# A gated recurrence with routed experts on one core: the first three groups in series, casts in 6 KB runs, the moduli row written transposed

## The chip, the cores and the metric

One core of a Trainium2 chip. The time is device microseconds of one execution of the program; the number given for a kernel is the median of its runs. A profile of one further execution shows which engine worked when.

## What is computed

For each of 4 batches and 8 heads a state of 48 x 48 complex numbers is decayed and turned at each of 768 steps by a gate (a_re, a_im), the outer product of k and v is added, and y is q times the real part. The 32 rows of heads then form x of 3072 tokens by 384, which goes through a top-1 mixture of 8 experts:

```python
mag = np.sqrt(a_re * a_re + a_im * a_im)
scale = np.minimum(mag, 0.999) / (mag + 1e-06)
a_re_n, a_im_n = (a_re * scale, a_im * scale)
for t in range(S):
    new_re = ar * S_re - ai * S_im
    new_im = ar * S_im + ai * S_re
    S_re, S_im = (new_re + k_t outer v_t, new_im)
    y[:, :, t] = q_t @ S_re
...
logits = x @ w_gate + modality_bias[modality_id]
e_idx = np.argmax(logits, axis=1)
out[mask] = gate_w[mask, None] * (np.maximum(x[mask] @ w1[e], 0.0) @ w2[e])
```

## The kernel before

**Units and groups.** The recurrence is cut into 6 chunks of 128 steps. A *unit* is one chunk of one batch with its 8 heads: 24 units, chunk by chunk. Two units make a *group* x (12 of them), and the element-wise work is done per group, on tiles of 128 steps by 768.

**Phases of a group.** `load_a` and `load_qk` (L100, L109) bring the inputs, four DMAs of 192 KB each, rows of 48 floats. `squares` (L116) makes the squared parts, `logs` (L127) their logarithms, `tangents` (L135) the tangent of the gate's angle, `arctans` (L148) the angle. `angles` (L151) sums the angles over the steps by a triangular matmul into PSUM tiles `u`; `fractions` (L171) takes the turns off, after adding the sum of the chunk before (`cb`, brought by `carries`, L162, from a DRAM row `f_scr` which `fractions` writes). `waves` (L193) makes sine and cosine (`cs`). `sums` and `moduli` (L201, L212) do the same with the log moduli and give `pm`. `moduli` also writes the last step's moduli to a DRAM row `m_scr` (L222) and reads it back with head and dimension exchanged, twice, into `mt` (L225), which scales the state.

**Stages of a unit.** `hats` (L232) multiplies q and k by moduli and waves. `turned` (L254) transposes both on TensorE (`tKT`, `tQT`), and ScalarE copies them to SBUF. `inner` (L266) makes the attention matrix (`wp`, then `W` by VectorE). `outer` (L279) makes the state's update (`up`) and the output (`yp`; after the first chunk also from the state, L302). `rows` (L307) transposes the output and computes the gate's logits (`xw`); ScalarE casts it into `xr` (L315), and a DMA writes it to `x_rows`.

**What sets the order.** ScalarE needs one set of function tables for log and exp and another for sine and arctan. `table` loads a set, and `then` chains table loads and activations into one order by hand. The loop over w (L360) interleaves: turn w runs `turned` of unit w + 2, `inner` of w + 1, `outer` of w, `rows` of w - 1, and phases of groups two to six ahead. Even turns use the log set, odd ones the sine set. Before the loop, groups 0 and 1 go through squares, logs and tangents together and then through arctans and angles together; the loop starts at w = -4, so that the first turns only have phases to do. Within this program order the framework's planner places each engine's instructions by when it reckons their inputs to be ready, and puts in the waits. SP issues all plain DMAs in one queue, in order; an instruction that waits holds those behind it.

**Casts.** `cast_weights` (L416) turns each expert's weights to bf16 in DRAM, 16 DMAs issued by GpSimd. `w1b` holds row k*128 + p of w1 in partition p, slot k; `w2b` row c*128 + p of w2. A cast is issued in two of three turns, and waits for a mark two turns back (L400 to L403).

**Experts.** After the router, 19 tiles (12 of 256 tokens, 7 of 128) run in `expert_layers` (L649): weights by DMA, tokens by gather, a transpose, `up` (L693: for each 128 hidden columns three matmuls with weights from `w1t`, into `h_ps`), `down` (L713, `y_ps`), and a scatter.

Of the kernel before, what the change touches and what calls it, by code (L numbers as in the profile page):

```python
# [11 lines left out]
F32 = mybir.dt.float32  # L12
BF16 = mybir.dt.bfloat16
# [6 lines left out]
U32 = mybir.dt.uint32  # L20
# [3 lines left out]
def gate_loop(nc, ctx, tc, cpool, ident, q, k, v, a_re, a_im, sel, lg, x_rows, casts, make_router):  # L24
# [4 lines left out]
    B, H, S, D = q.shape  # L29
    L = 128  # L30
    G = S // L
    J = H // 2
    C = 2 * D
    NG = 2
# [4 lines left out]
    un = ctx.enter_context(tc.tile_pool(name="un", bufs=2))  # L39
# [1 line left out]


    f_scr = nc.dram_tensor("f_scr", (G * B, H * D), F32, kind="Internal").ap()
    m_scr = nc.dram_tensor("m_scr", (G * B, H, D), F32, kind="Internal").ap()

    mask = cpool.tile([L, L], F32, name="mask")
    nc.gpsimd.memset(mask[:], 1.0)
# [14 lines left out]
    def bank(shape, name):  # L62

        full = ps.tile([128, 512], F32, name=name, tag="bank", bufs=7)
        n = 1
        for s in shape[1:]:
            n *= s
        flat = full[0:shape[0], 0:n]
        if len(shape) == 2:
            return flat  # L70
        names = " ".join(f"x{i}" for i in range(len(shape) - 1))
        return flat.rearrange(f"p ({names}) -> p {names}", **{f"x{i}": s for i, s in enumerate(shape[1:])})
# [7 lines left out]
    chain = []  # L80

    def then(ins):
        if chain:
            tc.add_manual_dep(ins.ins, chain[-1].ins.name, mybir.DependencyInfo(mybir.DependencyClass.NoSync, mybir.DependencyReason.DATA), reason="order of the table sets")
        chain.append(ins)

    def table(name):
        then(nc.scalar.preload_act_table_set(name))  # L88

    def act(*args, **kw):  # L90
        then(nc.scalar.activation(*args, **kw))  # L91
# [120 lines left out]
    def moduli(x):  # L212
        ls = box.pop(("sums", x))
        pm = el.tile([L, 2, NG, H, D], F32, name="pm")
        for i in range(NG):
            act(pm[:, 0, i], ls[i], Act.Exp)
            act(pm[:, 1, i], ls[i], Act.Exp, scale=-1.0)
        g, b = groups[x][0]
        if g < G - 1:

            n0 = g * B + b
            nc.sync.dma_start(out=m_scr[n0:n0 + NG].rearrange("i h d -> (i h d)")[None], in_=pm[L - 1:L, 0].rearrange("o i h d -> o (i h d)"))  # L222
            mt = un.tile([C, NG, H], F32, name="mt", bufs=4)
            for c in range(2):
                nc.sync.dma_start(out=mt[c * D:(c + 1) * D], in_=m_scr[n0:n0 + NG].rearrange("i h d -> d i h"))  # L225
            box["mt", x] = mt
        box["pm", x] = pm

    def both(x):
        return x[:, :, None, :].broadcast_to([L, H, 2, D])  # L230

    def hats(w):  # L232

        if not 0 <= w < NU:
            return
        x, i = w // NG, w % NG
        cs = box["cs", x]
        pm = box["pm", x]
        qk = box["qk", x]
        qp = un.tile([L, H, D], F32, name="qp")  # L240
        nc.vector.tensor_tensor(qp[:], qk[:, 0, i], pm[:, 0, i], Alu.mult)
        kp = un.tile([L, H, D], F32, name="kp")
        nc.vector.tensor_tensor(kp[:], qk[:, 1, i], pm[:, 1, i], Alu.mult)
        Kh = un.tile([L, H, 2, D], F32, name="Kh", bufs=5)
        nc.vector.tensor_tensor(Kh[:], cs[:, i], both(kp[:]), Alu.mult)
        Qh = un.tile([L, H, 2, D], F32, name="Qh", bufs=3)
        nc.vector.tensor_tensor(Qh[:], cs[:, i], both(qp[:]), Alu.mult)
        box["hats", order[w]] = Qh, Kh
# [58 lines left out]
    def rows(g, b):  # L307

        yT = box.pop(("outer", g, b))
        xw = bank([L, J, sel.shape[2]], "xw")  # L310
        for j in range(J):
            nc.tensor.matmul(xw[:, j, :], yT[:, j, :], sel[:, j, :], start=True, stop=True)  # L312
        nc.vector.tensor_reduce(lg[:, g * B + b, :], xw[:, :, C:].rearrange("t j e -> t e j"), axis=AX.X, op=Alu.add)
        xr = un.tile([L, J, C], BF16, name="xr")
        nc.scalar.copy(xr[:], xw[:, :, 0:C])  # L315
        n0 = 1 + (b * G + g) * L
        nc.sync.dma_start(out=x_rows[n0:n0 + L, 0:H * D // 2], in_=xr.rearrange("t j c -> t (j c)").bitcast(U32))

    NX = len(groups)
    NU = len(order)  # L320
    EXP, TRIG = "natural_log_exp_and_others", "trig_and_small"
    late = []
    takes = {7: 0, 15: 8, 19: 16, 23: 20}
    done = set()

    def phase(f, x):

        if 0 <= x < NX and (f, x) not in done:
            done.add((f, x))
            f(x)  # L330

    def unit(stage, w):
        if 0 <= w < NU:
            stage(*order[w])


    for x in range(2):
        phase(load_a, x)
    phase(load_qk, 0)
    phase(load_a, 2)  # L340
    table(EXP)
    for x in range(2):
        phase(squares, x)
        phase(logs, x)
        phase(tangents, x)
    table(TRIG)
    for x in range(2):
        phase(arctans, x)
        phase(angles, x)
    phase(fractions, 0)  # L350
    phase(squares, 2)
    phase(load_a, 3)
    phase(waves, 0)
    phase(load_qk, 1)
    phase(fractions, 1)

    rt = None
    open_ = []
    marks = []
    for w in range(-4, NU + 1):  # L360


        even = w % 2 == 0
        x = w // 2
        unit(values, w + 2)
        if even:
            phase(load_a, x + 6)
            phase(carries, x + 4)
            phase(fractions, x + 3)
        else:  # L370
            phase(load_qk, x + 3)
            hats(w + 3)
        unit(turned, w + 2)
        if even:
            if x + 2 < NX:
                table(EXP)
            phase(logs, x + 4)
        elif x + 3 < NX:
            table(TRIG)
            phase(arctans, x + 4)  # L380
        unit(inner, w + 1)
        if even:
            phase(sums, x + 2)
            phase(moduli, x + 2)
            for f in late:
                f(act)
            late.clear()
        unit(outer, w)
        if even:
            hats(w + 3)  # L390
            phase(tangents, x + 4)
        else:
            phase(waves, x + 3)
            phase(squares, x + 5)
        unit(rows, w - 1)
        if not even:
            phase(angles, x + 4)
        if w == 0:
            rt = make_router(ctx, ps, bank)
        marks.append(chain[-1])  # L400
        if casts and w >= 0 and w % 3 != 2:
            cast = casts.pop(0)()
            tc.add_manual_dep(cast.ins, marks[-3].ins.name, mybir.DependencyInfo(mybir.DependencyClass.Sync, mybir.DependencyReason.DATA), reason="spreads the casts over the turns")  # L403
        open_ = [t for t in open_ if next(t, True) is None]
        if w - 1 in takes:
            open_.append(rt.take(takes[w - 1], w, late))
            next(open_[-1])
# [7 lines left out]

def cast_weights(nc, moe_w1, moe_w2):  # L416

    E, Dt, F = moe_w1.shape
    w1b = nc.dram_tensor("w1b", (E, 128, Dt // 128, F), BF16, kind="Internal").ap()
    w2b = nc.dram_tensor("w2b", (E, 128, F // 128, Dt), BF16, kind="Internal").ap()  # L420
    casts = []
    for e in range(E):
        casts.append(lambda e=e: nc.gpsimd.dma_start(out=w1b[e], in_=moe_w1[e].rearrange("(k p) f -> p k f", p=128)))  # L423
        casts.append(lambda e=e: nc.gpsimd.dma_start(out=w2b[e], in_=moe_w2[e].rearrange("(c p) d -> p c d", p=128)))
    return w1b, w2b, casts


# [221 lines left out]
def expert_layers(nc, ctx, tc, identb, rt, x_rows, w1b, w2b, out):  # L649

    N, Dt = out.shape
    E = w1b.shape[0]
    F = w1b.shape[3]
    KD = Dt // 128
    NF = F // 128
# [37 lines left out]
    def up(w1t, xgT):  # L693
        n = xgT.shape[2]
        nf = 512 // n
        hT = fp.tile([128, NF, n], BF16, name="hT", bufs=2)
        for g in range(NF // nf):
            h_ps = pp.tile([128, nf, n], F32, name="h_ps", bufs=3)
            for f in range(nf):
                ff = g * nf + f  # L700
                for k in range(KD):
                    nc.tensor.matmul(h_ps[:, f, :], w1t[:, k, ff * 128:(ff + 1) * 128], xgT[:, k, :], start=(k == 0), stop=(k == KD - 1))  # L702
            if g % 2 == 0:
                nc.vector.tensor_relu(hT[:, g * nf:(g + 1) * nf], h_ps[:])  # L704
            else:
                nc.scalar.activation(hT[:, g * nf:(g + 1) * nf], h_ps[:], Act.Relu)  # L706
        return hT
# [25 lines left out]
    xgT = turn(got[0][0])  # L733
    for n, i in enumerate(order):
# [4 lines left out]
        if n + 1 < NTL:  # L739
            xgT = turn(got[n + 1][0])  # L740
# [75 lines left out]
```

## Time and profile before

| | us |
|---|---|
| median of 3 runs (416.97, 410.55, 416.11) | 416.11 |
| the profiled execution | 393.93 |
| its span, first to last instruction | 392.2 |
| TensorE busy | 328.1 (84%) |
| VectorE busy | 259.0 (66%) |
| ScalarE busy | 239.2 (61%) |
| GpSimd busy | 79.6 (20%) |
| DMA queue of SP, share of the 16 engines | 62.5% |
| DMA queue of GpSimd | 26.5% |

The page of the profile lists busy time of each engine, a strip of 40 slices, the chain of work that ended last, and groups of instructions by line. The timeline lists instructions in order of time: start, duration, engine, line, operation, output and input, how many were merged, and in brackets the idle time before and what ended it. PE is TensorE, PEld its weight loads, DVE VectorE, ACT ScalarE, POOL GpSimd, SPq the queue of SP; a DMA's duration there is the time its issue took, not the transfer. Pieces of the chain of waits have start, duration and what. A view by windows gives busy time of each engine in a stretch, the clock granted to TensorE and the share of the DMA engines in use (transfers can overlap, so it may pass 1). Matmul ends are modelled and overlap slightly.

### The profile page before, as it was taken

How to read it: one execution, taken by the hardware profiler on the slowest of the kernel's cores; microseconds unless marked ns; L12 is line 12 of the kernel's file. 1: busy time of each engine (PE TensorE's matmuls, PEld its weight loads, DVE VectorE, ACT ScalarE, POOL GpSimd, SP SyncE). 2: the span in 40 equal slices, each digit the busy share in tenths (PEclk: the TensorE clock that was granted, in tenths of full speed). 3: DMA queues.
4: the chain of work that ended last, by engine and by line, in shares of the span. 5: the costliest groups of instructions: out<-in, count | busy, mean ns of one | idle time of the engine just before them, and what ended most of it. 6: DMA issues, size and time to landing. Idle time of an engine off the chain costs nothing.

```text
span 392.2 us, 8756 instructions
## 1 busy us (share of the span) xinstructions
PE 328.1 (84%) x3381; PEld 269.9 (69%) x3381; DVE 259.0 (66%) x556; ACT 239.2 (61%) x386; POOL 79.6 (20%) x106
## 2 busy tenths in 40 slices
PE   0070949999999997899999999999407999999993
PEld 0030728788888886797979798999305777787772
DVE  2568797797969787997889789735632443443431
ACT  2859896989897978397979675352121333333331
POOL 5000010000000000000000011000045676776433
PEclk9996879999999999899999999999855999999999
DMA  9997599899899999979899993930169999999981
GB/s 145 187 152 173 91 163 184 125 195 195 150 222 159 184 166 217 185 126 147 184 181 186 153 160 64 185 69 13 30 245 365 404 404 413 405 407 406 411 357 40
DMA packets 173075, 80.89 MB, mean 206 GB/s; under 512 B 150387, under 2 KB 162152, under 8 KB 173034
## 3 DMA queue, kind: packets, MB, share of 16 engines
q1 hardware_dynamic: 158042, 59.97, 62.5%
q0 software_dynamic: 14992, 20.37, 26.5%
q8 instruction: 26, 0.43, 0.4%
q14 instruction: 15, 0.12, 0.1%
HBM read 85.75 MB, written 21.11 MB: 272 GB/s over the span
## 4 chain that ended last, share of the span: by engine, by line
PE 57%; ACT 11%; DMA 10%; issue 8%; POOL 4%; SPq 4%; DVE 4%; POOLq 0%; DVEq 0%; ACTq 0%
PE wp L273 9%; PE h_ps L702 7%; PE y_ps L713 6%; PE up L287 5%; PE xw L312 5%; PE yp L299 4%; DMA cb<-f_scr 4%; PE tQT L262 4%; PE yp L302 4%; PE tKT L262 4%; PE ls L207 4%; ACT sq L91 3%; PE u L157 3%; POOL out_dram L721 3%; ACT pm L91 2%
## 5 line engine op out<-in xcount | busy, mean ns | idle before, releaser
L157 PE MATMUL u<-tan,turn 128*128 128x384 f32 x48 | 24.4, 595 | 36.5 <-ACT tan L91 36.5
L273 PE MATMUL wp<-QT,KT 96*64 96x128 f32 x768 | 48.0, 278 | 1.7 <-DVE f L180 1.7
L273 PEld LDWEIGHTS wp<-QT,KT 96*64 96x64 f32 x768 | 42.2, 139 | 6.2 <-DVE f L180 2.7
L706 ACT ACTIVATE hT<-h_ps 128x512 bf16<-128x512 f32 x31 | 18.5, 597 | 45.6 <-PE h_ps L702 45.6
L702 PE MATMUL h_ps<-xgT,w1t 128*128 128x256 bf16 (+1 forms) x456 | 45.8, 259 | 0.0
L713 PE MATMUL y_ps<-w2t,hT 128*128 128x384 bf16 x248 | 43.5, 326 | 0.2 <-DVE hT L704 0.2
L702 PEld LDWEIGHTS <-w1t 128*128 128x128 bf16 x456 | 39.0, 100 | 5.9
L423 POOL DMA_DIRECT2D w1b<-in_moe_w_dram x8 | 5.9, 734 | 171.1 <-ACT off L91 86.3
L679 POOL DMA_INDIRECT xg<-x_rows,idx x31 | 30.0, 966 | 51.9 <-ACT idx L663 42.8
L157 PEld LDWEIGHTS u<-tan,turn 128*128 128x128 f32 x48 | 9.7, 230 | 41.2 <-issue 24.4
L721 POOL DMA_INDIRECT out_dram<-y_sb,idx x31 | 31.2, 1007 | 29.7 <-ACT y_sb L717 20.0
L299 PE MATMUL yp<-W,V 128*64 128x128 f32 x384 | 36.3, 277 | 0.0
L274 DVE TENSOR_TENSOR W<-wp,mask 128x512 f32<-128x512 f32 x48 | 32.3, 684 | 4.4 <-PE wp L273 4.3
L713 PEld LDWEIGHTS <-hT 128*128 128x128 bf16 x248 | 23.4, 98 | 14.1 <-DVE hT L704 0.3
L88 ACT ACT_TABLE_LOAD x25 | 32.1, 1283 | 1.2 <-PEq L800 0.8
L287 PEld LDWEIGHTS up<-V,Kh 128*96 128x96 f32 x320 | 29.5, 165 | 4.0 <-issue 2.7
L704 DVE TENSOR_SCALAR hT<-h_ps 128x512 bf16<-128x512 f32 x31 | 21.4, 692 | 16.0 <-PE h_ps L702 10.9
L302 PE MATMUL yp<-QT,state 96*48 96x128 f32 x320 | 31.1, 272 | 0.0
L287 PE MATMUL up<-V,Kh 128*96 128x48 f32 x320 | 30.4, 248 | 0.0
L263 ACT COPY KT<-tKT 96x512 f32<-96x512 f32 x48 | 25.8, 587 | 6.2 <-PE tKT L262 6.1
L304 ACT COPY yT<-yp 128x512 f32<-128x512 f32 x24 | 14.0, 585 | 22.7 <-PE yp L302 22.6
L312 PE MATMUL xw<-sel,yT 128*128 128x104 f32 x192 | 27.1, 285 | 0.0
(137 smaller groups left out, 653.3 us busy)
## 6 DMA issues: line engine op xcount, KB each, us to landing
w1t<-w1b SPq DMA_DIRECT2D x19, 768.0 KB, 12.0
w2t<-w2b SPq DMA_DIRECT2D x19, 768.0 KB
w1b<-in_moe_w_dram POOLq DMA_DIRECT2D x8, 768.0 KB, 7.6
w2b<-in_moe_w_dram POOLq DMA_DIRECT2D x8, 768.0 KB, 10.6
ab<-in_a_re_dram SPq DMA_DIRECT2D x24, 192.0 KB, 4.3
ab<-in_a_im_dram SPq DMA_DIRECT2D x24, 192.0 KB, 7.5
qk<-in_q_dram SPq DMA_DIRECT2D x24, 192.0 KB, 4.4
qk<-in_k_dram SPq DMA_DIRECT2D x24, 192.0 KB, 5.7
```

The costliest lines, as they stand in the source:

```text
L88: then(nc.scalar.preload_act_table_set(name))
L157: nc.tensor.matmul(u, turn[:], tan[:, i], start=True, stop=False)
L262: nc.tensor.transpose(tp[:, i, :], src[:, h4 + i].rearrange("t c d -> t (c d)"), ident[:])
L273: nc.tensor.matmul(wp[u * 64:(u + 1) * 64, i, :], KT[:, h4 + i, u * 64:(u + 1) * 64], QT[:, h4 + i, :], start=True, stop=True)
L274: nc.vector.tensor_tensor(W[:, h4:h4 + 4], wp, mask[:, None, :].broadcast_to([L, 4, L]), Alu.mult)
L287: nc.tensor.matmul(up[:, h, :], Kh[:, h].rearrange("t c d -> t (c d)"), V[:, h, 0:D], start=True, stop=True)
L299: nc.tensor.matmul(yp[u * 64:(u + 1) * 64, j, :], V[:, 2 * j + u, :], W[:, 2 * j + u, :], start=True, stop=(g == 0))
L302: nc.tensor.matmul(yp[u * 64:u * 64 + D, j, :], old[:, 2 * j + u, :], QT[:, 2 * j + u, :], start=False, stop=True)
L312: nc.tensor.matmul(xw[:, j, :], yT[:, j, :], sel[:, j, :], start=True, stop=True)
L702: nc.tensor.matmul(h_ps[:, f, :], w1t[:, k, ff * 128:(ff + 1) * 128], xgT[:, k, :], start=(k == 0), stop=(k == KD - 1))
L713: nc.tensor.matmul(y_ps[:], hT[:, f, s * 128:(s + 1) * 128], w2t[:, f, :], start=(f == 0), stop=(f == NF - 1))
L721: sc = nc.gpsimd.indirect_dma_start(out=out, out_offset=bass.IndirectOffsetOnAxis(ap=idx[:, s, 1:2], axis=0), in_=y_sb[:], in_offset=None, ...
```

## The change

Three things. First, groups 0, 1 and 2 go through their phases one after the other ahead of the loop, each with its switch of tables, and `turned` of units 0 and 1, `inner` and `outer` of unit 0 and hats 0 to 3 are placed between them. The loop starts at w = 0; its first two turns also take logs, tangents, arctans, angles and fractions of group 3. A set `done` keeps a stage from being done twice. Second, the casts read 12 KB and write 6 KB at a stretch: partition p now holds rows 3p to 3p + 2 of w1 and rows 8p to 8p + 7 of w2. The rows are padded by 32 elements. So that the products match, `rows` writes x with its columns permuted, and `up` takes every eighth hidden column as a chunk of weights. Third, `m_scr` is laid out transposed: its write scatters single words, and the two reads are contiguous.

```diff
-    m_scr = nc.dram_tensor("m_scr", (G * B, H, D), F32, kind="Internal").ap()
+    m_scr = nc.dram_tensor("m_scr", (G * B // NG, D, NG, H), F32, kind="Internal").ap()
...
-            nc.sync.dma_start(out=m_scr[n0:n0 + NG].rearrange("i h d -> (i h d)")[None], in_=pm[L - 1:L, 0].rearrange("o i h d -> o (i h d)"))
+            nc.sync.dma_start(out=m_scr[x].rearrange("d i h -> (i h) d")[None], in_=pm[L - 1:L, 0].rearrange("o i h d -> o (i h) d"))
...
-                nc.sync.dma_start(out=mt[c * D:(c + 1) * D], in_=m_scr[n0:n0 + NG].rearrange("i h d -> d i h"))
+                nc.sync.dma_start(out=mt[c * D:(c + 1) * D], in_=m_scr[x])
...
-        xr = un.tile([L, J, C], BF16, name="xr")
-        nc.scalar.copy(xr[:], xw[:, :, 0:C])
+        xr = un.tile([L, 3, J, C // 3], BF16, name="xr")
+        nc.scalar.copy(xr.rearrange("t k j q -> t j q k"), xw[:, :, 0:C].rearrange("t j (q k) -> t j q k", k=3))
...
+    for x in range(3):
+        table(TRIG)
         phase(arctans, x)
         phase(angles, x)
+        unit(values, x)
+        phase(load_a, x + 2)
+        phase(squares, x + 1)
+        phase(fractions, x)
+        unit(turned, x - 1)
+        unit(inner, x - 2)
+        phase(waves, x)
+        phase(load_qk, x + 1)
+        if x < 2:
+            table(EXP)
+            phase(sums, x)
+            phase(moduli, x)
+            hats(2 * x)
+            unit(turned, x)
+            unit(inner, x - 1)
+            phase(carries, 2)
+            phase(logs, x + 1)
+            phase(tangents, x + 1)
+            unit(outer, x - 1)
+            hats(2 * x + 1)
...
-    marks = []
-    for w in range(-4, NU + 1):
+    marks = [chain[-1], chain[-1]]
+    for w in range(NU + 1):
...
+            if w == 0:
+                phase(logs, 3)
+                phase(tangents, 3)
+                phase(squares, 4)
             phase(logs, x + 4)
         elif x + 3 < NX:
             table(TRIG)
+            if w == 1:
+                phase(arctans, 3)
+                phase(angles, 3)
+                phase(fractions, 3)
             phase(arctans, x + 4)
...
-    w1b = nc.dram_tensor("w1b", (E, 128, Dt // 128, F), BF16, kind="Internal").ap()
+    w1b = nc.dram_tensor("w1b", (E, 128, R + 32), BF16, kind="Internal").ap()[:, :, 0:R].rearrange("e p (k f) -> e p k f", f=F)
...
-        casts.append(lambda e=e: nc.gpsimd.dma_start(out=w1b[e], in_=moe_w1[e].rearrange("(k p) f -> p k f", p=128)))
-        casts.append(lambda e=e: nc.gpsimd.dma_start(out=w2b[e], in_=moe_w2[e].rearrange("(c p) d -> p c d", p=128)))
+        casts.append(lambda e=e: nc.gpsimd.dma_start(out=w1b[e], in_=moe_w1[e].rearrange("(p k) f -> p k f", p=128)))
+        casts.append(lambda e=e: nc.gpsimd.dma_start(out=w2b[e], in_=moe_w2[e].rearrange("(p c) d -> p c d", p=128)))
...
-                    nc.tensor.matmul(h_ps[:, f, :], w1t[:, k, ff * 128:(ff + 1) * 128], xgT[:, k, :], start=(k == 0), stop=(k == KD - 1))
+                    nc.tensor.matmul(h_ps[:, f, :], w1t[:, k].rearrange("p (m c) -> p c m", c=NF)[:, ff], xgT[:, k, :], start=(k == 0), stop=(k == KD - 1))
```

## The prediction

> **What bounds the kernel now.** I read first the page's 40 slices (9.8 us each), then TensorE's (PE) timeline, the chain of waits, SP's timeline, and the windows.
>
> ```profile
> PE   0070949999999997899999999999407999999993
> ACT  2859896989897978397979675352121333333331
> DMA  9997599899899999979899993930169999999981
> ```
>
> Three stages are visible: a start in which PE is mostly idle (slices 1 to 6), the gated recurrence up to about 280 us, and the expert layers from 298 us. In the recurrence PE is full, ScalarE (ACT) nearly so until slice 20, and the DMA engines are at nine tenths throughout. The PE timeline shows where "full" begins and where it breaks:
>
> ```profile
> 54.48 1.65 PE L157 MATMUL u<-tan,turn 128*128 128x384 f32 x2 [5.00 <-ACT tan L91]
> ...
> 57.84 1.91 PE L262 MATMUL tKT<-ident,Kh 128*96 128x128 f32 x8
> ...
> 158.11 0.17 PE L547 MATMUL rank<-acc,ones 128*128 128x8 bf16 x1 [3.26 <-DVE acc L526]
> ```
>
> From 54.48 on PE waits only 0.80, 0.50 and 0.40 us until 154; there it loses more, since a loss of 3.26 us is followed by work at the cold clock. The window 150 to 165 has 11.60 us of PE in 15.00. The chain of waits and SP's timeline name the cause:
>
> ```profile
> 148.62 8.72 DMA cb<-f_scr
> ...
> 157.43 0.56 DVE f L180
> ```
> ```profile
> 94.96 4.85 SPq L225 DMA_DIRECT2D mt<-m_scr  x2
> ...
> 147.51 1.07 SPq L106 DMA_DIRECT2D ab<-in_a_im_dram  x1
> 148.62 4.60 SPq L168 DMA_DIRECT2D cb<-f_scr  x1
> ```
>
> SP issues one DMA after another, each held up by full DMA engines; the carry `cb` leaves late and lands at 157.34, VectorE (DVE) sits behind it, and PE behind DVE. So up to 57 us a latency chain of ACT, DVE and PE bounds, then PE, with a DMA supply that just suffices.
>
> [...] the two `mt` loads carry 3 KB each and hold SP for 4.85 us at worst, 0.58 us each in the median. [...] The trace has only packed ones:
>
> ```profile
> 268.50 0.17 PE L545 MATMUL rank<-oneh,tri 128*128 128x8 bf16 x1
> 268.53 0.17 PE L547 MATMUL rank<-acc,ones 128*128 128x8 bf16 x1
> 268.56 0.17 PE L545 MATMUL rank<-oneh,tri 128*128 128x8 bf16 x1
> ```
>
> Each of these has its own 128x128 weight load and follows after 0.03 us: a packed load occupies no more than that.
>
> **The change, part by part.**
>
> *(a) The start in series.* Work is moved, none removed, so I lay the ACT order (chained by hand in `then`) against durations of the trace. Loads of group 0 are as before: squares to `off` run from 7.74 to 13.5. Round 0: table load 1.29, arctan 0.84: 15.7. From the arctan's end to the second bank of angles took 3.85 (54.42 to 58.27). Then 1.1 for two DVE steps, 1.76 for both sines, table 1.29, moduli 1.61: 25.3. Logs and exponentials of group 1 3.3, table 1.29, four copies of unit 0 2.15: 32.0. Round 1 the same (0.84 + 3.85 + 1.1 + 1.76 + 1.29 + 1.61 + 3.3 + 1.29 + 2.15 = 17.2): 49.2. Round 2: 0.84 + 3.85 + 2.05 (carry added) + 1.76: 57.7. The loop's first turn then has more than before ahead of `moduli` 2: table 1.29, logs and exponentials of group 3 3.3, copies of y and rows some 2.1, squares 4 1.48, its addition 0.97, logs 4 1.57, moduli 2 1.61: 70.0, against 67.4 in the trace (65.79 + 1.61). Group 3's sines follow after 1.7 + 1.29 + 1.6 + 3.85 + 2.05 + 1.76: 82.3, against 75.6. Group 3's moduli: squares 1.48, table 1.29, logs 1.6, moduli 1.61, copies of units 4 and 5 4.3: 92.6, against 85.1. Unit 6 needs both: after some 2.5 of DVE its transposes come at 95 to 96; in the trace they are at 94.22, where PE, not its input, set them.
>
> What PE has done by unit 6's transposes decides. If the planner that orders each engine's instructions fills PE's idle time, units 0 to 5 are complete by then, and against the trace at 94.22 that is extra: one `wp` 1.90, two `up` 2.9, two `yp` with state 3.75, three `xw` 2.95, less the angles of group 5 1.64: 9.9 us. With unit 6 at 95.5 the start gains 9.9 − 1.3 = 8.6 us. That is the best end: no slip in a chain of some forty handovers, ACT never late for another engine. If the planner keeps the program's order, `angles` 3 (ready at 74.6) stands ahead of `inner` 2 and PE idles until then; it has then done, beyond what stood at 57.84 in the trace, two units' transposes 3.5, `wp` 1.9, `up` and `yp` 2.45, moduli sums 1.7, less angles 1.64: 7.9 us, and restarts at half clock (`u` took 1.65 at 54.48 and 0.83 at 73.98), some 2 us: 74.6 + 2 − 7.9 − 57.8 = 10.9 lost. The trace shows filling (transposes stand between `rank` matmuls at 154 to 160, where those wait), so I expect most of it, with 0.1 us of slip per handover (4) and half a cold restart (1 to 2): 8.6 − 4 − 1.5 = 3, less a third of the way to the other end: about 0. Ends −9 and +11. SP: `carries` 3 and 4 and two `ab` loads now stand in one turn behind buffers that squares 3 and 4 free; with those at 52 and 66 the carries are in by about 75, before the 78 at which they are read. If late, each us falls on unit 6. The first two casts now wait for one mark and leave together at about 60, 7 us apart before; the loads of groups 5 and 6 have some 10 us of room.
>
> *(b) Casts.* 16 casts of 768 KB stay. Between 100 and 150 four casts ran and the software queue had 33.9% of the DMA engines: 17 us, 4.2 each; over 80 to 250 it is nearer 4.7. Runs grow from 4 KB and 1.5 KB read (2 KB and 0.75 KB written) to 12 and 6. The expert stage moves 6 KB runs at 406 GB/s, so 1.5 MB read takes at least 3.8 us: up to 0.9 saved per cast, 1.2 us per pair of units; lower bound 0 or a little loss[...].
>
> *(c) Moduli row.* 1536 single-word reads become 768 single-word writes and 96 reads of 64 B. SP's median 2 x 0.58 shrinks to about 2 x 0.35, the 0.25 of the write grows to 0.6: even. In DMA time about half of the words go; if one costs what a 192 B packet does (1024 of them, 192 KB at 187 GB/s: 1.03 us), 0.7 us per pair. Against it: SP waits for the write before `mt` (6 waits, 7.7 us in all now), and a write of words may be later by 1 to 3 us.
>
> (b) and (c) matter where DMA is late: the 5 to 6 us at 154 to 160, and 1.7 in three gaps. I take 2.5 saved; ends 6 and −3.
>
> *(d) Row copy with a permuted output:* 24 copies of 0.479. Same elements; if single 2-byte writes halve the rate, 0.4 x 24 = 10 us of ACT, spread over units in which ACT has 42.91 of 50 us. I take 0 on the path; ends 0 and 3.
>
> *(e) Strided weights of `up`:* 456 loads, one element in 16 bytes. In the chain of waits 24 `up` matmuls with their loads take 2.62 us at 256 columns and 1.34 at 128: 109 and 56 ns per pair. A load of up to 56 ns costs nothing; the packed one is at 0.03 us, so even half its rate hides. At 107 ns it costs 7 tiles x 24 x 51 ns = 8.6 us; at 213 ns, 12 x 24 x 104 + 7 x 24 x 157 ns = 56 us. I take 0[...]. The padded rows change no run length of the weight loads (6 KB): 0.
>
> Sum: 0 − 2.5 = −2.5 on the profiled execution's 393.93 (span 392.2 and 1.7 around it): 391.4. The runs' median is 416.11, 22 us above it; nothing in the change touches that difference, so 413.6, say 413.
>
> **Rivals.**
> 1. *The head start holds* (faster): PE is dense from unit 4 on and keeps 8.6; with 3 to 5 of the DMA stall that is −12 to −13: 404. For it: ACT has 36 us idle between 70 and 250, so it can follow. Against it: the same ACT chain bounds the start.
> 2. *PE stands behind angles 3* (slower): the program's order is kept where ACT's first loop turn is long; +10.9 − 2.5: 424. It decides if `inner` 2 starts after 74 and unit 6's transposes after 104. For it: from 57.84 to 78 the trace's PE follows the program's order exactly. Against it: there PE had no idle time to fill.
> 3. *Strided loads show* (slower): 107 ns per load in `up`, +8.6 − 2.5: 422. It decides once a load exceeds 56 ns. [...] Against it: 0.03 us for a packed load.
>
> That casts and row do nothing is within the forecast: 416.
>
> **Chances.** Forecast (405 to 420) 0.48; rival 1 0.26; rival 2 0.16; rival 3 0.10. Within 2% (8.3 us, about what a measurement of this kernel can tell, its three runs spread by 6.4) means 407.8 to 424.4. Faster: rival 1 and a sliver of the forecast, 0.29; slower: rival 2 and 3 where they lack the 2.5 or meet the costs of (d), 0.25 with the forecast's far end; same 0.46. Range for 8 in 10: 401 (rival 1 with all of the stall) to 428 (rival 2 or 3 with the cost of (d)).
>
> **What would show it.** (a) right: unit 0's transposes near 27 instead of 42, PE idle of 6 to 10 us between 60 and 78, unit 6's transposes at 95 to 101. Wrong upward past 104, or if PE breaks again before 110. (b): the software queue's share between 100 and 150 below 0.30. (c): `mt` issue under 0.45 us each, no `cb` piece over 5 us in the chain. (d): `xr` mean near 0.48. (e): 24 `up` matmuls in 2.62 and 1.34 us. The forecast is wrong altogether if the expert stage from its first `h_ps` to the end, 94 us now, grows by more than 4, or if two casts at once delay the loads of groups 5 and 6.

## The result, and the profile after

The changed kernel takes 465.38 us (median of 4 runs, 461.79 to 472.33) against 416.54 us for the kernel before beside it (4 runs, 410.55 to 418.4): 1.123 times, 95% interval 1.098 to 1.148. I had forecast 413, with a range up to 428. The prediction was wrong, in sign and in size. Here and below a ratio is estimated from the fast runs of both kernels (those within 1.5% of the kernel's fastest), while the medians take all runs, so a ratio need not be the quotient of the medians.

The profiled execution took 463.09 us, its span 461.4. The same three rows of the 40 slices (11.5 us each) as shown of before:

```profile
PE   0546727599988798897689998999129798789991
ACT  3698693489974889595498995475222222223321
DMA  9969699497888789499769987830199999989920
```

PE works earlier (5 in the second slice), but falls to 2 in the sixth, and its nines are broken up until slice 25, where before they nearly ran through. In the chain of waits (start, duration, what) the long pieces are new, and they are one DMA:

```profile
76.94 9.40 DMA m_scr<-pm
87.27 2.08 DMA mid<-in_moe_modality_id_dram
...
129.40 10.78 DMA m_scr<-pm
...
251.61 15.68 DMA m_scr<-pm
268.62 6.87 DMA qk<-in_k_dram
```

These three writes of the moduli row, 3 KB each, take 9 to 16 us to land (the chain of before has one, of 5.76), and what follows the first and the last is a load that stood behind it. SP's waits (total, times, longest) say the same; first the line of before, then that of the changed kernel:

```profile
SPq L225 <- DMA m_scr<-pm: 7.7, 6, 2.2
```
```profile
SPq L224 <- DMA m_scr<-pm: 53.1, 9, 8.1
```

ScalarE's row copy is the other surprise, 1895 ns in the mean where it was 475 (columns of the group: busy, mean ns, then idle time before it):

```profile
L315 ACT CAST xr<-xw 128x384 bf16<-128x384 f32 x24 | 11.4, 475 | 7.0 <-DVE lg L313 6.3 <-DMA mt<-m_scr 0.7
```
```profile
L315 ACT CAST xr<-xw 128x384 bf16<-128x384 f32 x24 | 45.0, 1895 | 22.2 <-DVE lg L313 21.8
```

And TensorE's start is late, as my second rival had it:

```profile
72.30 1.65 PE L157 MATMUL u<-tan,turn 128*128 128x384 f32 x2 [11.39 <-ACT tan L91]
...
90.63 3.68 PE L273 MATMUL wp<-QT,KT 96*64 96x128 f32 x32 [5.12 <-DVE f L180]
...
109.54 1.04 PE L262 MATMUL tKT<-ident,Kh 128*96 128x128 f32 x8
```

The last of these are unit 6's transposes, which the kernel before has at 94.22:

```profile
94.22 1.04 PE L262 MATMUL tKT<-ident,Kh 128*96 128x128 f32 x8
```

The first product of the experts starts at 345.15 us against 298.26, so 47 us are lost before the expert stage. From there to the last scatter it takes 108.0 us against 89.2, 19 more. At most 2 of these 19 turned out to belong to the change (below).

### The profile page after: what moved, and what is told of

Read it like the earlier page. It is cut to its first block, busy times and chain, and to the rows that moved or that the text cites. A ratio compares the mean times of both kernels' runs of the same rounds, so it can differ in the third digit from the quotient of the medians.

```text
span 461.4 us, 8757 instructions
## 1 busy us (share of the span) xinstructions
PE 354.3 (77%) x3381; PEld 288.1 (62%) x3381; DVE 259.1 (56%) x556; ACT 270.9 (59%) x386; POOL 75.5 (16%) x106
## 4 chain that ended last, share of the span: by engine, by line
PE 41%; DMA 19%; ACT 12%; SPq 11%; issue 8%; DVE 4%; POOL 3%; another core or an unknown queue 1%; POOLq 0%; DVEq 0%; ACTq 0%
DMA m_scr<-pm 8%; PE h_ps L729 7%; PE y_ps L740 6%; PE wp L273 5%; SPq L106 4%; DMA qk<-in_k_dram 4%; DMA cb<-f_scr 3%; PE xw L312 3%; PE up L287 3%; PE yp L299 3%; PE ls L207 3%; ACT sq L91 3%; SPq L224 2%; PE yp L302 2%; PE tKT L262 2%
## 5 line engine op out<-in xcount | busy, mean ns | idle before, releaser
L273 PE MATMUL wp<-QT,KT 96*64 96x128 f32 x768 | 51.5, 290 | 9.6 <-DVE f L180 9.5
L315 ACT CAST xr<-xw 128x384 bf16<-128x384 f32 x24 | 45.0, 1895 | 22.2 <-DVE lg L313 21.8
L273 PEld LDWEIGHTS wp<-QT,KT 96*64 96x64 f32 x768 | 45.1, 145 | 14.9 <-DVE f L180 10.5
L729 PEld LDWEIGHTS <-w1t 128*128 128x128 bf16 x456 | 44.5, 146 | 11.2 <-issue 9.3
L740 PE MATMUL y_ps<-w2t,hT 128*128 128x384 bf16 x248 | 47.3, 335 | 4.3 <-ACT hT L733 2.3
L287 PEld LDWEIGHTS up<-V,Kh 128*96 128x96 f32 x320 | 32.3, 177 | 14.6 <-ACT xr L315 11.0
L287 PE MATMUL up<-V,Kh 128*96 128x48 f32 x320 | 33.1, 260 | 9.8 <-ACT xr L315 9.7
L299 PE MATMUL yp<-W,V 128*64 128x128 f32 x384 | 38.4, 290 | 0.0
L263 ACT COPY KT<-tKT 96x512 f32<-96x512 f32 x48 | 31.0, 687 | 6.9 <-PE tKT L262 6.9
L262 PE MATMUL tKT<-ident,Kh 128*96 128x128 f32 x192 | 27.8, 289 | 5.3 <-DVE Kh L245 5.2
```

Source lines behind the costliest of these rows:

```text
L262: nc.tensor.transpose(tp[:, i, :], src[:, h4 + i].rearrange("t c d -> t (c d)"), ident[:])
L273: nc.tensor.matmul(wp[u * 64:(u + 1) * 64, i, :], KT[:, h4 + i, u * 64:(u + 1) * 64], QT[:, h4 + i, :], start=True, stop=True)
L287: nc.tensor.matmul(up[:, h, :], Kh[:, h].rearrange("t c d -> t (c d)"), V[:, h, 0:D], start=True, stop=True)
L299: nc.tensor.matmul(yp[u * 64:(u + 1) * 64, j, :], V[:, 2 * j + u, :], W[:, 2 * j + u, :], start=True, stop=(g == 0))
L315: nc.scalar.copy(xr.rearrange("t k j q -> t j q k"), xw[:, :, 0:C].rearrange("t j (q k) -> t j q k", k=3))
L729: nc.tensor.matmul(h_ps[:, f, :], w1t[:, k].rearrange("p (m c) -> p c m", c=NF)[:, ff], xgT[:, k, :], start=(k == 0), stop=(k == KD - 1))
```

## The experiments

Kernels of one set ran on one chip beside the kernel before. The sets were not all on the same chip; in them the kernel before took 395.5, 416.7, 414.8, 414.3 and 416.4 us. So I compare ratios, and times only within a set.

### First set: each part alone

**Order alone** (the diff of the loop and of `unit` and `hats`, nothing else).

> The kernel before with the new order of the first three groups alone. Theory A (each of the three parts costs its own): the planner keeps the program's order, PE stands behind the angles of later groups, so the transposes of unit 6 come at 104 to 110 us instead of 94, and the time is 8 to 15 us over that of before; the row copy stays at 0.48 us, the expert stage at 90 to 94 us. Rival B (the late start seen in the changed kernel comes from the write of the moduli row, which holds the queue of SP and so brings carries and values late): unit 6 at 94 to 98 us, the time within 4 us of before.

**Row alone** (the three lines with `m_scr`).

> The kernel before with the transposed moduli row alone. Theory A: every write of 768 single words takes 9 us or more to land although the DMA engines have room, SP waits for it before the reads, and what stands behind in its queue (values, carries, loads) comes late: waits of SP for the write of 45 to 55 us in sum against 7.7, time 5 to 20 us over before. Rival C (the wait hides, since SP issues far ahead of need): the same long waits of SP, but the time within 4 us.

**Casts alone** (`cast_weights`, `xr`, and the weights of `up`).

> The kernel before with the casts alone, and what belongs to them: 6 KB runs, rows padded by 64 bytes, the row copy with permuted output, weights of up taken one in eight. Theory A: the row copy takes 1.9 us, 34 us more of ScalarE over 24 units, of which 15 to 25 us reach PE, and the expert stage takes 105 to 109 us against 90 to 94: 30 to 40 us over before. Rival D (ScalarE has room for the copy, only the expert stage costs): 12 to 18 us over before, gate part as before. Rival E (the expert stage is slow only because the gate part left something late): 15 to 25 us over before and an expert stage of 90 to 94 us.

**Casts, with the permutation made by `sel`**, the constant that transposes x's columns back:

```diff
-        nc.scalar.copy(xr.rearrange("t k j q -> t j q k"), xw[:, :, 0:C].rearrange("t j (q k) -> t j q k", k=3))
+        nc.scalar.copy(xr.rearrange("t k j q -> t j k q"), xw[:, :, 0:C].rearrange("t j (k q) -> t j k q", k=3))
...
-        nc.gpsimd.tensor_copy(sel[u * 64:u * 64 + D, :, u * D:(u + 1) * D], ident[u * 64:u * 64 + D, None, u * 64:u * 64 + D].broadcast_to([D, H // 2, D]))
+        nc.gpsimd.tensor_copy(sel[u * 64:u * 64 + D, :, 0:2 * D].rearrange("p j (k q) -> p j q k", k=3)[:, :, u * 16:(u + 1) * 16], ident[u * 64:u * 64 + D, u * 64:u * 64 + D].rearrange("p (q k) -> p q k", k=3)[:, None].broadcast_to([D, H // 2, 16, 3]))
```

> As the kernel with the casts alone, but the permutation of x's columns is made by the selection matrix, so the row copy writes runs of 32 elements (64 bytes). Theory A: the copy is back at 0.48 to 0.6 us, the gate part within 5 us of before, the expert stage still 105 to 109 us: 12 to 18 us over before. Rival D: no difference from the kernel with the casts alone (within 4 us). If the copy stays near 1.9 us, its time is not set by the order of its writes.

| kernel | us (before: 395.54) | ratio, 95% interval | expert stage, us |
|---|---|---|---|
| order | 400.93 | 1.017 (1.010 to 1.023) | 88.6 |
| row | 444.23 | 1.119 (1.107 to 1.130) | 88.6 |
| casts | 401.45 | 1.014 (1.007 to 1.022) | 90.7 |
| casts, `sel` | 399.67 | 1.012 (1.006 to 1.018) | 89.9 |

The row alone is the result: 49 us, far over the 5 to 20 us that its theory A expected. Order and casts cost 5 to 6 us each. For the casts, theory A's 30 to 40 us was wrong, as were rival D's 12 to 18 and rival E's 15 to 25; the order came out between its two texts, with unit 6 late (104.50) as theory A had it. SP's waits in the kernel with the row alone:

```profile
SPq L225 <- DMA m_scr<-pm: 61.4, 10, 8.2
```

Its SP timeline shows one write. V and half of q are issued behind it, then SP stands until 58.87:

```profile
49.62 0.56 SPq L222 DMA_DIRECT2D m_scr<-pm  x1
50.23 0.63 SPq L252 DMA_DIRECT2D V<-in_v_dram  x1
50.91 1.58 SPq L112 DMA_DIRECT2D qk<-in_q_dram  x1
58.87 0.97 SPq L225 DMA_DIRECT2D mt<-m_scr  x2
```

The windows over that wait (length, PE busy, clock, share of the DMA engines, GB/s):

```profile
49.60:52.00 2.40, 1.05 (x20) 1.00 0.66 185
52.00:54.00 2.00, 0.00 (x0) 1.00 0.45 29
54.00:56.00 2.00, 0.36 (x1) 0.76 0.35 30
56.00:58.80 2.80, 2.80 (x7) 0.56 0.23 24
58.80:62.00 3.20, 3.20 (x43) 1.00 0.79 134
```

V and the half of q, 384 KB, are two microseconds of work at 185 GB/s. They trickle at 24 to 30 GB/s, with the engines in use a quarter to a half of the time, until the words have landed. The other nine writes look alike: by SP's timeline the reads, which wait for the landing, follow the ten writes after 9.2 to 14.1 us, in the kernel before after 1.4 to 5.8. So there are two suspects: SP, which issues nothing, and the transfers behind the words, which hardly move.

### Second set: what it is about the row

**The changed kernel again**, unaltered.

> The changed kernel itself once more, beside the parts of it. Theory A (the parts add: row +49 us, order +5, casts +6): 1.13 to 1.16 times before, and the expert stage (first h_ps to the last scatter) takes 88 to 92 us as in every part so far, so that the 108 us of its first profile belonged to that execution. Rival I (the three together make a slow expert stage that no part has): 105 us or more again in the expert stage.

**The changed kernel with the row of before.**

> The changed kernel with the moduli row as before: written as one stretch, read word by word. Theory A: all but order and casts is given back, so 1.02 to 1.04 times before; unit 6's transposes at 103 to 107 us, the row copy still 1.9 us. Rival I: the expert stage stays over 105 us and the time over 1.06 times before.

**Row alone, read one turn later**: the two loads of `mt` move from `moduli` into a phase of their own.

```diff
+    def bring(x):
...
+            nc.sync.dma_start(out=mt[c * D:(c + 1) * D], in_=m_scr[x])
...
             phase(load_qk, x + 3)
+            phase(bring, x + 2)
```

> The kernel before with the transposed row, and its two reads issued one turn later, so that SP needn't stand behind the write. Theory H (the cost is SP's hold: it issues nothing for 6 us): waits of SP for the write fall from 61 to under 20 us and the time comes to within 10 us of before, or 1.025 times. Rival J (the words clog the DMA engines or the memory behind them, and whatever was issued behind them trickles until they are done): SP's waits fall, but the loads issued behind the write still land late, and 25 us or more of the 49 remain.

**Row alone, words 64 bytes apart.**

```diff
-    m_scr = nc.dram_tensor("m_scr", (G * B // NG, D, NG, H), F32, kind="Internal").ap()
+    m_scr = nc.dram_tensor("m_scr", (G * B // NG, D, NG, H, 16), F32, kind="Internal").ap()[:, :, :, :, 0]
```

> The kernel before with the transposed row, but [...] as many words are written, none beside another, and the two reads are of single words again as before. Rival K (the write is slow [...]): the write lands in 3 to 5 us instead of 11, and the time comes to within 10 us of before. Theory L (each single-word write has its price wherever it goes): landing stays at 9 us or more and the time at 1.10 times before or above, as the word reads come on top.

| kernel | us (before: 416.69) | ratio, 95% interval | expert stage, us |
|---|---|---|---|
| changed, again | 473.45 | 1.134 (1.119 to 1.150) | 113.4 |
| changed, row of before | 426.71 | 1.024 (1.012 to 1.037) | 111.3 |
| row, read later | 464.3 | 1.110 (1.095 to 1.125) | 114.0 |
| row, words apart | 426.25 | 1.027 (1.015 to 1.039) | 111.1 |

SP's wait in front of the reads (theory H) is out. With the reads a turn later SP stands behind the write for 7.9 and 2.0 us only, and still 11% are lost. The windows of that kernel over one write, issued at 48.12, show that what is queued behind the words is late whether SP waits for them or not (SP can't run far ahead there either: issuing half of q takes it 7.91 us at 56.04):

```profile
52.00:54.00 2.00, 0.00 (x0) 0.54 0.89 64
54.00:56.00 2.00, 1.87 (x4) 0.50 0.49 23
56.00:58.00 2.00, 2.00 (x7) 0.50 0.55 25
58.00:60.00 2.00, 2.00 (x15) 0.75 0.93 146
```

A price per word (theory L) is out too. Just as many words, 64 bytes apart, cost 2.7% instead of 11.9%, SP's waits fall to a fifth, the reads follow the writes after 4.7 to 8.6 us (rival K had 3 to 5), and after one write (issued at 48.22) the rate is back at 141 GB/s in the window 3 to 5 us later:

```profile
SPq L225 <- DMA m_scr<-pm: 12.5, 9, 2.9
```
```profile
49.40:51.40 2.00, 0.00 (x0) 1.00 0.15 15
51.40:53.40 2.00, 0.00 (x0) 0.79 0.85 141
53.40:55.40 2.00, 1.16 (x2) 0.50 1.08 180
```

The kept traces also list each packet of the DMA engines, and there the two layouts hardly differ at first. After the write at 49.62 (words side by side) nearly all 768 words start on the engines 1.2 to 3.9 us after the issue, after the one at 48.22 (words apart) 1.2 to 4.1 us after it, and most take 7 ns each. Yet the reads follow 9.2 us after the first and 4.7 us after the second. So the time is lost after the engines have handled the words; what holds it up there, no view shows.

The changed kernel with the row of before is back at 1.024, so the row costs 11% here too. The expert stage of 108 us is hardly a matter of the change. All four kernels of this set need 111 to 114, two of them with that stage's code untouched, so rival I is out as well; all four of the first set need 88.6 to 90.7, the casts 1 to 2 us more than the others. In one window of 50 us inside the stage (busy of PE, PEld, DVE, ACT, POOL, clock, DMA share, GB/s), the row alone on the first chip:

```profile
350.00:400.00 50.00, 50.00 (x453) 38.50 (x451) 22.10 (x36) 16.99 (x32) 33.19 (x35) 0.98 1.02 404
```

and the changed kernel on the second:

```profile
400.00:450.00 50.00, 44.10 (x368) 33.05 (x367) 17.16 (x29) 14.03 (x24) 24.82 (x25) 0.97 0.94 330
```

The DMA engines stay in use, but move 330 GB/s instead of 404. The profile of before that I predicted from had 404 to 413: that fits the first chip, and its runs of 410 to 417 us fit the second. This is where the 22 us between its profiled execution and its median come from, as far as the runs show it. Whether it is the chip itself or something else that ran on it, no run tells.

### Third set: dose, copy, weights, and an edit of before

**Words 16 bytes apart**: the same line as for 64 bytes, with 4 in place of 16.

> The kernel before with the transposed row and its words 16 bytes apart[...]; the reads are of single words. Theory K ([...] the price grows with their number): between the two measured ends, 1.03 and 1.12, nearer the lower: 1.04 to 1.06, the longest wait of SP for the write 3.5 to 6 us. Rival S [...]: 1.10 or more, waits up to 8 us. Rival T (compact reads were what hurt, not the writes): 1.02 to 1.03 as with words 64 bytes apart.

**The copy in the order of its output**, in the kernel with the casts alone:

```diff
-        nc.scalar.copy(xr.rearrange("t k j q -> t j q k"), xw[:, :, 0:C].rearrange("t j (q k) -> t j q k", k=3))
+        nc.scalar.copy(xr[:], xw[:, :, 0:C].rearrange("t j (q k) -> t k j q", k=3))
```

> The kernel with the casts alone, where ScalarE's row copy runs through the same elements in the order of its output: it writes 2-byte elements one beside the other and reads its input in PSUM at every third word. Theory O (the order of the writes set the 1.9 us): 0.45 to 0.7 us per copy, and the time of the kernel with the selection matrix, 1.005 to 1.018 times before. Rival P (a strided side on either end costs as much): over 1.5 us per copy.

**Only w1 cast in 6 KB runs, weights of `up` packed** (`w2` as before, `sel` permuted).

> The kernel before with the casts of w1 alone in 6 KB runs, the permutation of x's columns in the selection matrix; w2 is cast as before, so up's weights are packed again. Theory M (what is left over of 1.2% in the kernel with both casts and the selection matrix comes from the strided weight loads, 146 ns against 100): weight loads back at 100 ns and a time of 0.993 to 1.003 times before. Rival N (it comes from the long packets of the casts[...]): 1.006 to 1.015 times before.

**The kernel before with `bring`**, and nothing of the change.

> The kernel before with one thing changed that no part of the change has: the two reads of the moduli row are issued one turn after its write. Theory Q (SP's 7.7 us behind the write, in turns where the carry is late, cost PE part of its 5 to 6 us at 154 to 160): 2 to 5 us faster, 0.987 to 0.995 times before. Rival R (that stall comes from full DMA engines alone): within 0.5% of before.

| kernel | us (before: 414.82) | ratio, 95% interval |
|---|---|---|
| row, words 16 bytes apart | 429.01 | 1.035 (1.027 to 1.043) |
| casts, copy in order of output | 417.35 | 0.997 (0.992 to 1.003) |
| w1 alone, packed | 417.42 | 1.005 (1.000 to 1.011) |
| before, read later | 419.48 | 0.999 (0.994 to 1.004) |

Four words in 64 bytes: SP waits 18.7 us in all, 3.9 at most.

```profile
SPq L225 <- DMA m_scr<-pm: 18.7, 9, 3.9
```

With 16, 4 and 1 word in 64 bytes SP waits 61.4, 18.7 and 12.5 us, and the ratio is 1.119, 1.035 and 1.027 (the first on another chip than the other two). The order is what theory K expects, a price that grows with the number of words in 64 bytes, but the time came out below its 1.04; rival S, with 1.10 or more, is out. Rival T, which blames the compact reads, has the time nearly right, but cannot explain SP's waits: they end before any read is issued.

The copy's time is set by the order of its writes, not by a stride on either side. Reading PSUM at every third word and writing side by side takes what the plain copy took (the line's own view: least, median, greatest ns); below it the same elements in the order of the change, from the kernel with the casts alone:

```profile
L315 ACT CAST xr<-xw x24: 464/471/502, 77.4 to 278.8; 128x384 bf16<-128x384 f32 x24
```
```profile
L315 ACT CAST xr<-xw x24: 1852/1886/2217, 77.3 to 282.3; 128x384 bf16<-128x384 f32 x24
```

Packed weights of `up` load in 100 ns, strided ones in 146. Whether either is seen in the time isn't settled: 1.005 with the packed, 0.997 with the strided, and neither theory M's range nor rival N's contains 1.005. Issuing the reads of before a turn later gains nothing; rival R holds.

### Fourth and fifth set: the order

The kernel with the order alone already has the late start. Its TensorE timeline shows PE standing behind the angles of group 3:

```profile
74.07 1.65 PE L157 MATMUL u<-tan,turn 128*128 128x384 f32 x2 [12.65 <-ACT tan L91]
...
77.57 2.21 PE L274 MATMUL wp<-QT,KT 96*64 96x128 f32 x32
...
104.50 1.04 PE L263 MATMUL tKT<-ident,Kh 128*96 128x128 f32 x8
```

**Angles of group 3 behind `outer`:**

```diff
                 phase(arctans, 3)
-                phase(angles, 3)
-                phase(fractions, 3)
...
         unit(outer, w)
+        if w == 1:
+            phase(angles, 3)
+            phase(fractions, 3)
```

> The new order alone, with the angles and fractions of group 3 moved behind the second turn's outer, so that TensorE's program has inner of unit 2 and outer of unit 1 ahead of them. Theory U (the start is late because TensorE stands in program order behind the angles of group 3): its idle piece of 12.65 us at 61 to 74 shrinks to 5 to 9 us, the transposes of unit 6 come at 97 to 101 us instead of 104.5, and the time is 0.998 to 1.008 times before instead of 1.017. Rival V (ScalarE's chain sets when the start ends, whatever stands first on TensorE): unit 6 at 102 us or later and 1.012 times before or more.

**The whole change with row, copy and angles mended.**

> The whole change with its three costs taken out: moduli row as before, angles of group 3 behind outer, row copy in the order of its output. Theory A (costs add, and what is left are the gains I forecast): 0.985 to 1.0 times before. Rival W (there was nothing to gain: the order costs what it saves and the casts were hidden): 1.0 to 1.01.

**The kernel before with casts, copy in order of output, and `bring`.**

> The kernel before with the casts in 6 KB runs, the row copy in the order of its output, and the two reads of the moduli row one turn later, the two edits that came out at 0.997 and 0.999 times before. If both gain a little, 0.993 to 0.997 times before; if neither does, 0.998 to 1.002.

They came to 1.015 (1.006 to 1.023), 1.024 (1.015 to 1.034) and 1.028 (1.020 to 1.036) times before, 414.29 us here. The second and third lie above everything that was expected of them. Of the first, theory U has the idle piece right, 7.94 us instead of 12.65, and the rest wrong: unit 6's transposes stay at 105.24, and both marks of rival V are met. VectorE's timeline of that kernel shows the next obstacle: it waits for the router's token ids in the middle of group 3's fractions:

```profile
76.83 0.56 DVE L180 TENSOR_TENSOR f<-u,cb 128x384 f32<-128x384 f32 x1
83.51 0.18 DVE L510 TENSOR_SCALAR is_m<-mid 128x24 f32<-128x24 int32 x1 [6.12 <-DMA mid<-in_moe_modality_id_dram]
...
84.88 0.55 DVE L180 TENSOR_TENSOR f<-u,cb 128x384 f32<-128x384 f32 x1
```

In the order alone the same wait is 4.16 us, in the kernel before 2.75, outside its start. The router is made in turn 0, which the new order puts right into the start, and its loads stand on SP behind four loads of `ab`.

**The router made later**, with the order alone:

```diff
-        if w == 0:
+        if w == 5:
             rt = make_router(ctx, ps, bank)
```

> The new order alone, with the router made five turns later (its first use is in turn 8), so that its small loads, which stood on SP behind four held loads, and VectorE's reading of them no longer stand in the start. Theory X (VectorE waits 4.16 us for the ids, in program order ahead of the second half of group 3's fractions, and ScalarE and TensorE after it): the transposes of unit 6 at 98 to 101 us instead of 104.5, and 0.999 to 1.008 times before instead of 1.017. Rival V (ScalarE's chain is the end of the start, whatever the ids do): unit 6 at 103 us or later, 1.012 or more.

**Router later and angles behind `outer`.**

> The new order alone, with the router made five turns later and the angles of group 3 behind outer. Theory X with U (what filling gave was lost again behind the ids, where VectorE waited 6.12 us): unit 6 at 96 to 100 us, 0.993 to 1.004 times before. Rival V: unit 6 at 103 us or later, 1.012 or more.

**The same with casts, and the copy in order of output.**

> As the one before, with the casts in 6 KB runs and the row copy in the order of its output; the moduli row as in the kernel before. If the casts gain where DMA is late, 0.985 to 1.0 times before; if they are hidden or cost a little, as in two of three kernels so far, 1.0 to 1.02.

| kernel | us (before: 416.39) | ratio, 95% interval |
|---|---|---|
| order, router later | 417.52 | 1.006 (1.003 to 1.009) |
| and angles behind `outer` | 414.75 | 0.995 (0.992 to 0.998) |
| and casts | 417.88 | 1.004 (1.001 to 1.008) |

With the router alone moved, VectorE no longer waits for the ids in the start, but the idle piece stays at 12.40 us and unit 6 at 104.27, so theory X's mark is missed. The ratio is lower than the order's, but on another chip. With both edits and the casts, unit 6 starts 4 us earlier:

```profile
75.26 1.65 PE L157 MATMUL u<-tan,turn 128*128 128x384 f32 x2 [7.95 <-ACT tan L91]
...
100.25 1.04 PE L262 MATMUL tKT<-ident,Kh 128*96 128x128 f32 x8
```

The second kernel of this set, without the casts, does not show it. In its profile (an execution of 418.8 us) VectorE now stands behind the ids at 91 to 96 us, and unit 6 is as late as in the order alone, though unit 5 is 4.7 us earlier (90.93):

```profile
96.07 0.18 DVE L510 TENSOR_SCALAR is_m<-mid 128x24 f32<-128x24 int32 x1 [4.75 <-DMA mid<-in_moe_modality_id_dram]
...
104.73 1.92 PE L263 MATMUL tKT<-ident,Kh 128*96 128x128 f32 x8
```

So removing one obstacle showed the next. This second kernel is 0.5% faster than before, the only one whose interval lies below 1; that an earlier start is what gains it isn't shown.

What the casts lose against it, 3.1 us in the medians, has a place in the traces: a DRAIN of GpSimd, an instruction with which it closes its program; the span ends 0.8 us after it in both kernels shown. Here are the kernel before and the one with the casts alone (least, median and greatest ns of the three at that line):

```profile
L811 POOLq DRAIN  x3: 46/110/4237, 387.2 to 392.0; - x3
```
```profile
L814 POOLq DRAIN  x3: 46/110/7667, 394.1 to 402.3; - x3
```

Every profile of a kernel with both casts in 6 KB runs has 7.67 us there, every one with the casts of before 4.24, and the one with only w1 changed 3.22. So 3.4 us, 0.8% of the time, are lost after the last product, whatever the casts save earlier. Why this instruction takes longer isn't shown.

## Why the prediction was wrong, step by step

**(c) Moduli row: the step that failed.** I had SP "even", 0.7 us of DMA time saved per pair of units, and the write "later by 1 to 3 us". The issues came near the reckoning: the reads hold SP for 0.414 us each in the median, where I had 0.35, and the write for 0.555, where I had 0.6. What failed is the landing, and what stands behind it. In the changed kernel the reads follow the ten writes after 8.7 to 15.7 us, before after 1.4 to 5.8: in the mean 7 us later, not 1 to 3. Meanwhile the transfers behind the write trickle, for which the sum had no term. In the sum, −2.5 for casts and row should have been about +49 for the row alone. I counted words and their engine time, and priced a written word like a read one. The single-word writes in the trace of before, the 128 gate weights of a tile (`gw`), lie 772 bytes apart and land in 2.0 us in the median, so they don't bound words side by side; my upper end (+3) was taken from waits of a write in one stretch. I also asked only what stands behind the write on SP, not what stands behind it in the DMA engines. My two signs for this part split: the issues of `mt` stayed under 0.45 us, but a `cb` of 11.18 us stands in the chain, where I had none over 5. The closer the words lay, the more the kernel lost (1.119, 1.035 and 1.027 at 4, 16 and 64 bytes, the first on another chip); no run here shows why.

**(a) Order: centre wrong, cause half known.** Forecast 0 with ends −9 and +11; measured +1.7% (1.0 to 2.3), some 6.6 us of 395.5. Unit 6's transposes came 10.3 us late, at 104.50, and `inner` of unit 2 at 77.57: both marks of rival 2, whose price was +10.9 without the 2.5. Between unit 6 and unit 23 the kernel then takes 163.2 us (104.50 to 267.74) instead of 167.8 (94.22 to 262.03), so 4.6 come back, about what PE had lost at 154 to 160 (it waited 3.26 us there, and the granted clock was 0.70 in 158 to 160 and 0.50 in 160 to 162). I had said that the planner would fill PE's idle time, from transposes that stand between `rank` matmuls; it kept the program's order here. The paper schedule was right up to unit 0 (27 forecast, 26.94) and for `moduli` 2 (end at 70.0 forecast, 70.3). It broke at the sines of group 3: end forecast at 82.3, measured at 87.4. In between stands the router's `mid`, which I never listed, though each DMA that a moved step is moved past was to count. It is not all of it: with the router moved away, the sines still end 14.9 us after `moduli` 2, where I had 12.3 and the order alone has 17.1.

**(b) Casts: saving right, worth nothing, and a cost at the end not listed.** With the casts alone the software queue has 22.4% of 402.5 us against 26.5% of 392.2, that is 13.8 us less for 16 casts: 0.86 each, my upper end of 0.9. In time this showed in no kernel, and the longer DRAIN at the end takes 3.4 us, for which I had no term. My sign for the saving, a share below 0.30 between 100 and 150, was met with the casts alone (0.249, from the packets) and missed in the changed kernel (0.408), where the casts moved no more bytes but their packets took longer.

**(d) Row copy: size wrong.** 0.475 us became 1.895, 34 us more of ScalarE where my upper bound was 10: I let scattered 2-byte writes halve the rate, an assumption that no trace of before backed, and they quartered it. Beside the kernel with `sel` it costs 1.8 us in the medians (401.45 against 399.67), which their intervals don't tell from nothing, so the ends 0 and 3 stand. The trace of the casts alone has 4.2 us of waits of PE and its loads behind it. The 21.0 us of them in the changed kernel (the matmuls' and the loads' waits added, so partly the same time) stand in a stage that was late already.

**(e) Strided weights: right to within 1 us.** 146 ns per load instead of 100; that strided loads cost nothing was not shown by any trace of before, and the 0.03 us I set beside it is the spacing of packed loads that overlap, each of 0.10 us. 24 `up` matmuls take 2.62 us at 256 columns as before, and 1.47 to 1.49 instead of 1.34 at 128: about 7 × 0.14 = 1 us. That is 61 to 62 ns per pair of load and matmul, just past the 56 where I had the cost begin, and far from the 107 that rival 3 assumed; its 8.6 us are out.

**My last criterion misled.** I wrote that the forecast was wrong altogether if the expert stage grew by more than 4 us. It grew by 22, from 94.0 to 116.2; 19 of these stand before the last scatter and are nearly all the chip or what ran on it, and the other 3.4 are the DRAIN of the casts.

**What stays open.** How close is too close for written words: 4, 16 and 64 bytes were tried, nothing between or beyond, and the words 64 bytes apart still cost 2.7%. Why the casts with `bring` gave 1.028 when each gave 0.997 and 0.999 in another set: the quotients of the medians over all runs, 1.020 against 1.006 and 1.011, hardly disagree, so part of it may lie in the estimate. Why the DRAIN is longer: no line of the traces explains it.

## What to carry to other kernels

Price a transfer on its write side too: here, turning a strided read into a scattered write of single words moved the cost to where it held up what was queued behind, and the row alone took 11.9% more time. When a step is moved earlier, walk each in-order queue at the new place, small constant loads and the vector work that reads them included; where two instructions stand in the way, removing one shows only the next. Look at the time after the last product too: here 3.4 us were lost there, whatever the casts saved earlier. And compare a profile with times of the same chip, or read each stage against a kernel that leaves it untouched.

## What the runs showed of the hardware

- After 768 words written side by side across 3 KB of DRAM the DMA engines stay at 24 to 30 GB/s for some 6 us in the write shown; with 64 bytes between the words, 141 GB/s are back 3 to 5 us after the issue. The reads that wait for the landing follow after 9.2 to 14.1 and 4.7 to 8.6 us.
- ScalarE writes 384 bf16 elements per partition in 0.47 us side by side and in 1.89 us with 256 bytes between neighbours: 3.7 ns more per element, four times as long in all. Reading PSUM 12 bytes apart cost it nothing (0.471 us against 0.479).
- A 128x128 bf16 weight load with 16 bytes between elements takes 146 ns, a packed one 100.
- The same stage streams its weights at 404 GB/s on one chip and at 330 on another: 89 to 91 us become 108 to 114 in two sets there, and 106 to 108 on two more.
- The DRAIN of GpSimd that ends the program takes 4.24 us with the casts of before and 7.67 with both in 6 KB runs, in every profile.
